# First W_down piece in DMAs of 8, 8 and 112 rows, and c and x in DMAs of odd row counts, in a decode block on one core

## The chip, the cores and the metric

The kernel runs on one core of a Trainium2 chip. The metric is device time in microseconds (us) of one execution. Times below are medians of the runs in the fast state unless said otherwise. (In the slow state an execution is over 1.5% above the fastest of the same kernel.) The profile of the kernel before is of one further execution of 440.03 us.

## The reference

One decode step of a transformer block for 8 batch rows, with adaptive layer norm (six modulation vectors from `c`), grouped-query attention over a cache, and a gated ReLU MLP. Cut to what matters:

```python
mod = (silu(c) @ w_mod)                      # 1024 x 6144
h = layernorm(x) * (1 + ca) + sa
x = x + ga * attention(h, k_cache, v_cache, wq, wo)   # caches: 8 x 4 x 8192 x 128 each
h = layernorm(x) * (1 + cb) + sb
gate, up = h @ W_gate, h @ W_up              # 1024 x 3584 each
x = x + gb * (((gate > 0) * gate * up) @ W_down)      # 3584 x 1024
```

There are only 8 rows of activations, so nearly all the work is reading 185.6 MB of bf16 caches and weights from HBM once.

## The kernel before

All large loads pass through one ring in SBUF (`arena`), in a fixed order: w_mod, wq, then K and V of 16 pairs, wo, W_gate and W_up in two pieces each, W_down in five pieces that get smaller. Each load is one DMA over 128 partitions. They are issued from one queue, as far ahead as the ring has room:

```python
def pump():
    while stream:
        key, src, n = stream[0]
        lo = cursor[0] if cursor[0] + n <= RING else 0
        if P.unread("arena", lo, lo + n):
            return
        ...                                   # cut
        dst = arena[:, lo:lo + n]
        ...                                   # cut
        P.op("sp", lambda e, dst=dst, src=src: e.dma_start(dst, src), writes=[slot_r(lo, lo + n)], dma=True)
...                                           # cut
d_src = B_W_down.rearrange("(p k) n -> p (k n)", k=KF)      # 28 rows of W_down in each partition
...
wd_parts = [(0, 14), (14, 21), (21, 25), (25, 27), (27, 28)]
for i, (r0, r1) in enumerate(wd_parts):
    load(("wd", i), d_src[:, r0 * D:r1 * D], (r1 - r0) * D)
```

So the first W_down piece has 128 rows of 28 KB, the others rows of 14, 8, 4 and 2 KB. A "row" below is what one partition gets from one DMA; in the trace it is one packet (128 packets of 14336 bytes for the second W_down piece, 640 of 28672 for the five loads with 28 KB rows). `c` and `x` are 32 rows of 512 bytes each, queued behind the first half of w_mod.

## Time and profile before

| | before |
|---|---|
| median of 3 runs, the slow one of 446.05 included | 439.97 us (439.25 to 446.05) |
| profiled span | 438.7 us |
| HBM read | 185.6 MB, 423 GB/s over the span |
| a 32 KB row / a 28 KB row on its engine (packet records) | 1.213 us / 1.062 us |
| last W_down piece landed | 435.4 us |

From the page of the kernel before: the span; the busy share of the 16 DMA engines in 40 slices, in tenths; what they moved in each slice; the queues; and the chain that ended last, by engine and by line.

```profile
span 438.7 us, 4012 instructions
DMA  8999999999999999999999999999999999999994
GB/s 359 433 421 444 436 433 429 434 430 429 430 433 430 429 430 430 432 436 434 436 432 433 445 432 430 430 430 432 430 429 428 430 432 437 434 430 430 431 425 180
q1 hardware_dynamic: 6896, 185.64, 98.4%
q8 instruction: 13, 0.21, 0.2%
PE 35%; DMA 32%; DVE 26%; ACT 4%; issue 2%; SPq 1%
PE ps L482 18%; DMA arena<-in_A_k_cache_dram 15%; PE ps L439 13%; DVE kt L428 10%; DMA arena<-in_A_wq_dram 9%; DMA arena<-in_B_W_down_dram 8%; DVE pT L473 7%; DVE negm L446 4%; ACT prb L466 4%; PE ps L452 1%; PE ps L571 1%; DVE mj L457 1%; PE ps L375 1%; PE ps L592 1%; DVE mjt L460 1%
```

The DMA engines are busy from the first slice to the last, at about 430 GB/s. The chain names PE first, but from the first K on a load is issued 25 us and more before it lands (medians by tensor, 25.1 to 36.0 us), so the DMA engines never run dry for long on account of PE. What counts is the end, in the timeline of the kernel before (start, duration, engine, line, operation; in brackets the idle time of the engine before it and what ended that):

```profile
417.49 3.18 PE L592 MATMUL ps<-arena,hT 128*32 128x448 bf16 x32 [5.27 <-DMA arena<-in_B_W_up_dram]
425.96 2.98 PE L610 MATMUL ps<-arena,kt 128*32 128x256 bf16 x56 [5.30 <-DMA arena<-in_B_W_down_dram]
430.26 0.95 PE L610 MATMUL ps<-arena,kt 128*32 128x256 bf16 x28 [1.32 <-DMA arena<-in_B_W_down_dram]
433.63 1.04 PE L610 MATMUL ps<-arena,kt 128*32 128x256 bf16 x16 [2.42 <-DMA arena<-in_B_W_down_dram]
434.86 1.02 PE L610 MATMUL ps<-arena,kt 128*32 128x256 bf16 x12 [0.18 <-DMA arena<-in_B_W_down_dram]
435.93 0.42 DVE L614 TENSOR_TENSOR lu<-ps,mod 128x256 f32<-128x256 f32 x1 [12.25 <-PE ps L610]
```

Every group of matmuls waits for its DMA. After the last piece only a fixed tail is left.

The semaphore of each of these loads gets 16 updates, read here as one from each engine; those of the last piece spread over 4.08 us.

### The profile page before, as it was taken

What the parts mean: (1) busy time and instruction counts of PE and PEld (TensorE: products, weight loads), DVE (VectorE), ACT (ScalarE), POOL (GpSimd) and SP (SyncE); (2) the same over time, 40 slices, a digit from 0 to 9 for tenths busy, and PEclk for the clock granted to TensorE, in tenths of its full rate; (3) what the DMA queues carried; (4) which work ended last, traced back from release to release, by engine and by line L of the source; (5) the groups of instructions that cost most, each with busy time, mean ns of one, the idle gap of its engine ahead of it and who ended that gap; (6) DMA issues with size and microseconds to landing.
All of it is one profiled execution on the core that took longest, in us unless ns stands there. A gap on an engine that the chain in (4) does not pass through costs nothing.

```text
span 438.7 us, 4012 instructions
## 1 busy us (share of the span) xinstructions
PE 271.6 (62%) x1691; PEld 121.2 (28%) x1691; DVE 263.6 (60%) x372; ACT 28.8 (7%) x48; POOL 19.8 (5%) x77
## 2 busy tenths in 40 slices
PE   0053446759595866859586776859586685655243
PEld 0021112324242332324233332424233242342021
DVE  0143057787687867778596867869687878430020
ACT  1100012010101011010101001010101101100000
POOL 6000010000000000000000000000000000000000
PEclk9997669697888969698796968888798978685556
DMA  8999999999999999999999999999999999999994
GB/s 359 433 421 444 436 433 429 434 430 429 430 433 430 429 430 430 432 436 434 436 432 433 445 432 430 430 430 432 430 429 428 430 432 437 434 430 430 431 425 180
DMA packets 6946, 185.90 MB, mean 424 GB/s; under 512 B 816, under 2 KB 912, under 8 KB 1168
## 3 DMA queue, kind: packets, MB, share of 16 engines
q1 hardware_dynamic: 6896, 185.64, 98.4%
q8 instruction: 13, 0.21, 0.2%
q14 instruction: 5, 0.04, 0.0%
q10 hardware_dynamic: 32, 0.01, 0.0%
HBM read 185.63 MB, written 0.02 MB: 423 GB/s over the span
## 4 chain that ended last, share of the span: by engine, by line
PE 35%; DMA 32%; DVE 26%; ACT 4%; issue 2%; SPq 1%
PE ps L482 18%; DMA arena<-in_A_k_cache_dram 15%; PE ps L439 13%; DVE kt L428 10%; DMA arena<-in_A_wq_dram 9%; DMA arena<-in_B_W_down_dram 8%; DVE pT L473 7%; DVE negm L446 4%; ACT prb L466 4%; PE ps L452 1%; PE ps L571 1%; DVE mj L457 1%; PE ps L375 1%; PE ps L592 1%; DVE mjt L460 1%
## 5 line engine op out<-in xcount | busy, mean ns | idle before, releaser
L428 DVE STREAM_TRANSPOSE kt<-arena 128x1024 uint32<-128x1024 uint32 x128 | 149.1, 1215 | 40.4 <-DMA arena<-in_A_k_cache_dram 33.1
L439 PE MATMUL ps<-kt,qpad 128*128 128x512 bf16 x512 | 120.8, 382 | 10.0 <-DVE kt L428 8.7
L482 PE MATMUL ps<-arena,pT 128*64 128x512 bf16 x512 | 94.0, 547 | 51.1 <-DVE pT L473 51.1
L482 PEld LDWEIGHTS ps<-arena,pT 128*64 128x64 bf16 x512 | 44.8, 155 | 94.5 <-issue 89.7
L439 PEld LDWEIGHTS ps<-kt,qpad 128*128 128x128 bf16 x512 | 45.5, 97 | 83.7 <-DVE kt L428 26.5
L473 DVE STREAM_TRANSPOSE pT<-prb 64x1024 bf16<-64x1024 bf16 x32 | 39.6, 1239 | 15.9 <-ACT prb L466 15.4
L466 ACT ACTIVATE prb<-ps,bias 128x1024 bf16<-128x1024 f32 x16 | 17.8, 1113 | 275.0 <-DVE mjt L460 275.0
L446 DVE TENSOR_REDUCE negm<-ps 128x1 f32<-128x512 f32 x32 | 22.1, 689 | 11.7 <-PE ps L439 11.7
L421 POOL COPY qpad<-qR 32x32 bf16<-32x32 bf16 x64 | 13.0, 203 | 308.2 <-PE ps L439 253.8
L592 PE MATMUL ps<-arena,hT 128*32 128x448 bf16 x128 | 12.7, 577 | 14.5 <-DMA arena<-in_B_W_up_dram 6.8
L452 PE MATMUL ps<-identf,negm 128*128 128x128 f32 x32 | 7.8, 325 | 15.7 <-DVE negm L450 15.7
L495 DVE SCALAR_TENSOR_TENSOR om<-ps,im,om 128x128 f32<-128x128 f32 x48 | 16.7, 347 | 0.6
L599 DVE TENSOR_TENSOR kt<-ps,kt 128x448 bf16<-128x448 f32 x2 | 1.2, 619 | 25.0 <-PE ps L592 25.0
L500 PE MATMUL ps<-jmp,om 128*128 128x16 f32 x32 | 6.5, 279 | 14.7 <-DVE om L495 14.7
L375 PE MATMUL ps<-arena,hT 128*32 128x512 bf16 x64 | 6.9, 608 | 13.9 <-DMA arena<-in_A_wq_dram 13.9
L290 DVE CAST cxr<-ps 128x512 bf16<-128x512 f32 x1 | 0.7, 692 | 19.6 <-PE ps L288 19.6
L288 PE MATMUL ps<-cx,rsel 32*128 32x512 bf16 x1 | 0.6, 581 | 19.0 <-DMA cx<-in_A_x_dram 19.0
L610 PE MATMUL ps<-arena,kt 128*32 128x256 bf16 x112 | 6.0, 372 | 9.2 <-DMA arena<-in_B_W_down_dram 9.2
L452 PEld LDWEIGHTS ps<-identf,negm 128*128 128x128 f32 x32 | 4.7, 186 | 23.6 <-DVE negm L450 22.1
L385 DVE CAST kt<-ps 128x512 bf16<-128x512 f32 x1 | 0.7, 692 | 17.2 <-PE ps L375 17.2
L592 PEld LDWEIGHTS ps<-arena,hT 128*32 128x32 bf16 x128 | 4.5, 139 | 22.0 <-DMA arena<-in_B_W_up_dram 8.4
L500 PEld LDWEIGHTS ps<-jmp,om 128*128 128x128 f32 x32 | 5.0, 195 | 18.0 <-DVE om L495 16.9
(80 smaller groups left out, 94.7 us busy)
## 6 DMA issues: line engine op xcount, KB each, us to landing
arena<-in_A_k_cache_dram SPq DMA_DIRECT2D x16, 4096.0 KB, 28.2
arena<-in_A_v_cache_dram SPq DMA_DIRECT2D x16, 4096.0 KB, 25.1
arena<-in_w_mod_dram SPq DMA_DIRECT2D x2, 6144.0 KB, 17.8
arena<-in_A_wq_dram SPq DMA_DIRECT2D x2, 4096.0 KB, 20.0
arena<-in_A_wo_dram SPq DMA_DIRECT2D x2, 4096.0 KB, 26.9
arena<-in_B_W_gate_dram SPq DMA_DIRECT2D x2, 3584.0 KB, 29.4
arena<-in_B_W_up_dram SPq DMA_DIRECT2D x2, 3584.0 KB, 32.5
arena<-in_B_W_down_dram SPq DMA_DIRECT2D x1, 3584.0 KB, 36.0
```

The costliest lines, as they stand in the source:

```text
L375: fns.append(lambda e, w=w, z=z, g=g, kk=kk: e.matmul(ps[32 * g:32 * g + 32, 3 + z, :], hT[:, kk, :], w[:, g, z, :], start=(kk == 0), stop ...
L421: P.op("pool", lambda e, n=2 * m + Q // 2, Q=Q: e.tensor_copy(qpad[32 * Q:32 * Q + 32, m % 2, :, 24 + 32 * Q:32 + 32 * Q], qR[32 * Q:32 * ...
L428: P.op("dve", lambda e: e.transpose(ktb[:, to:to + QE].bitcast(dt.uint32), arena[:, lo:lo + QE].bitcast(dt.uint32)), reads=[slot_r(lo, lo ...
L439: fns.append(lambda e, t=t, r=r: e.matmul(ps[:, b, :].rearrange("p (c k) -> p c k", k=32), qpad[:, m % 2, t * 2 + r, 24 - 8 * i:152 - 8 * ...
L446: P.op("dve", lambda e: e.tensor_reduce(negm[:, h:h + 1], ps[:, b, :], AX.X, ALU.max, negate=True), reads=[bank(b)], writes=[R("negm", h, ...
L452: P.op("pe", lambda e: e.matmul(ps[:, 4, 0:128], negm[:, 2:3].to_broadcast([128, 128]), identf[:], start=True, stop=True), reads=[R("negm" ...
L466: P.op("act", lambda e: e.activation(prb[:], ps[:, 2 * z:2 * z + 2, :].rearrange("p h n -> p (h n)"), ACT.Exp, bias=bias[:, z:z + 1], scal ...
L473: P.op("dve", lambda e, g=g: e.transpose(pT[64 * g:64 * g + 64, z, :, g, :], prb[64 * g:64 * g + 64, :]), reads=[R("prb"), R("pT", z, z + ...
L482: fns.append(lambda e, t=t: e.matmul(ps[64 * (t % 2):64 * (t % 2) + 64, 5, :].rearrange("p (i d) -> p i d", d=Dh), pT[:, z, t].rearrange(" ...
L495: P.op("dve", lambda e, i=i: e.scalar_tensor_tensor(out=om[:], in0=ps[:, 5, Dh * i:Dh * i + Dh], scalar=im[:, i:i + 1], in1=om[:], op0=ALU ...
L500: P.op("pe", lambda e: e.matmul(ps[:, 6, 16 * m:16 * m + 16], om[:], jmp[:].rearrange("p g j -> p (g j)"), start=True, stop=True), reads=[ ...
L592: fns.append(lambda e, w=w, r=kk - r0, kk=kk, h=h, j=j, b0=b0: e.matmul(ps[32 * j:32 * j + 32, b0 + h, 0:H], hT[:, kk, :], w[:, r, j, h, : ...
```

## The change

Its intent: let half of the DMA engines carry 9 of the rows of the first W_down piece and the other half 7, so that all end together; and give c and x a ramp of row counts over the engines. As far as the traces show it, a DMA of 8 rows runs on 8 engines and one of 112 on 16. The core of the diff (the rest lets one operation hold several DMAs on one semaphore):

```diff
-        def load(key, src, n):
-            stream.append((key, src, n))
+        def load(key, src, n, cuts=(0, 128)):
+            stream.append((key, src, n, cuts))
...
-                P.op("sp", lambda e, dst=dst, src=src: e.dma_start(dst, src), writes=[slot_r(lo, lo + n)], dma=True)
+                P.op("sp", [lambda e, a=a, b=b, lo=lo, n=n, src=src: e.dma_start(arena[a:b, lo:lo + n], src[a:b])
+                            for a, b in zip(cuts, cuts[1:])], writes=[slot_r(lo, lo + n)], dma=True)
...
-            load(("wd", i), d_src[:, r0 * D:r1 * D], (r1 - r0) * D)
+            load(("wd", i), d_src[:, r0 * D:r1 * D], (r1 - r0) * D, (0, 8, 16, 128) if i == 0 else (0, 128))
...
-            P.op("sp", lambda e, t=t, src=src: e.dma_start(cx[:, t, :], src), writes=[R("cx", t, t + 1)], dma=True)
+            cuts = ((0, 13, 24, 31, 32), (0, 15, 24, 29, 32))[t]
+            P.op("sp", [lambda e, t=t, src=src, a=a, b=b: e.dma_start(cx[a:b, t, :], src[a:b])
+                        for a, b in zip(cuts, cuts[1:])], writes=[R("cx", t, t + 1)], dma=True)
```

More of the change, by code (lines that the diff above doesn't have):

```diff
@@ L77, in op @@
         if dma:
-            o["dma"] = self.n_dma
+            o["dma"] = self.n_dma % self.N_DMA_SEMS
             self.n_dma += 1
@@ L100, in plan @@
         count = {e: 0 for e in self.ENGINES}
+        landed = [0] * self.N_DMA_SEMS
         for i, o in enumerate(self.ops):
@@ L103, in plan @@
             if o["dma"] is not None:
-                o["sem"] = ("dma", o["dma"] % self.N_DMA_SEMS)
-                o["val"] = 16 * (o["dma"] // self.N_DMA_SEMS + 1)
+                landed[o["dma"]] += 16 * len(o["fns"])
+                o["sem"] = ("dma", o["dma"])
+                o["val"] = landed[o["dma"]]
             elif o["inc"]:
@@ L126, in emit @@
                 ins = f(e)
-            if o["dma"] is not None:
-                ins.then_inc(sems[o["sem"]], 16)
-            elif o["inc"]:
+                if o["dma"] is not None:
+                    ins.then_inc(sems[o["sem"]], 16)
+            if o["inc"]:
                 ins.then_inc(sems[o["sem"]], 1)
@@ L220, in bass_adaLN_cond__gqa_block_cached__glu_gated_reglu__decode_kernel @@
         stream, place, cursor = [], {}, [0]
-        def load(key, src, n):
-            stream.append((key, src, n))
+        def load(key, src, n, cuts=(0, 128)):
+            stream.append((key, src, n, cuts))
         def pump():
             while stream:
-                key, src, n = stream[0]
+                key, src, n, cuts = stream[0]
                 lo = cursor[0] if cursor[0] + n <= RING else 0
@@ L233, in pump @@
                 place[key] = lo
-                dst = arena[:, lo:lo + n]
-                if len(src.shape) == 3:
-                    dst = dst.rearrange("p (a n) -> p a n", a=src.shape[1])
-                P.op("sp", lambda e, dst=dst, src=src: e.dma_start(dst, src), writes=[slot_r(lo, lo + n)], dma=True)
+                P.op("sp", [lambda e, a=a, b=b, lo=lo, n=n, src=src: e.dma_start(arena[a:b, lo:lo + n], src[a:b])
+                            for a, b in zip(cuts, cuts[1:])], writes=[slot_r(lo, lo + n)], dma=True)
         wm_src = w_mod.rearrange("(p k) n -> p (k n)", k=KC)
```

## The prediction

> **What bounds the kernel now.** DMA. The page's slices show the DMA engines at 9 tenths in all but the first and last. In the packet records a 32 KB row takes 1.213 us and a 28 KB row 1.062 us on its engine, practically without spread, so each engine runs at 27.0 GB/s; 185.6 MB over 16 engines at that rate take 429.5 of the 438.7 us. The chain of waits ends with the W_down pieces: the last of them lands at 435.4 us, then matmuls, two DVE operations (0.42 us each) and the output stores, 3.3 us in all. So the last engine's finish sets the time, not the mean.
>
> **Where engines differ.** A DMA's semaphore gets one update per engine, so the landings show skew. The 16 updates of the first load lie within 1.4 us; those of the last piece are, from its first: 0, 0.14, 0.23, 0.26, 0.44, 0.78, 0.85, 1.49, 1.78, 1.88, 2.52, 3.04, 3.05, 3.06, 3.16, 4.08 us. There are 13 instruction packets of 16 KB (DMA queue table), each about 0.95 us, and about each one coincides with one engine dropping back by some 1.5 us. [...]roughly half of the engines are 2 to 3 us behind. Mean lag 1.7 us, worst 4.1 us.
>
> **What the change does.** [...]the 8-row output stores have 9 updates where others have 16. So each 8-row piece puts one row on engines 0 to 7, and the 112-row piece 7 rows on every engine. Against 8 rows now, the low half gains 1.06 us and the high half loses 1.06 us. The c and x rows (0.027 us each, 4 per engine) become a ramp from 8 on engine 0 to 0 on engine 15: 0.1 us either way. SP gains 8 issues of 0.4 us; loads are issued over 25 us ahead and W_mod streams until 16.8 us, so that is hidden.
>
> **Worth.** If the laggards are the high half, the last landing moves from 4.08 to about 3.0: -1.0 us, all on the critical chain. If they are the low half: +1.1 us.
>
> **The risk.** [...]+6 to +13 us. I give this about 0.4.
>
> **Prediction.** 439.5 us, range 438.0 to 449.5; faster by over 2%: 0.01, within 2%: 0.78, slower by over 2%: 0.21.
>
> **What would show it.** Right: W_down rows of 28 KB stay at 1.06 us and the last piece's landings close up to about 3 us or less. Port sharing: those rows take 2 to 4 us and first W_down lands many us later.
>
> **What would make it wrong.** Laggards not lying in one half; instruction packets falling on other engines; port sharing milder or harsher.

The forecast came to 439.5 us, in a range of 438.0 to 449.5. "Port sharing" is the name for the theory that engines slow one another when they write certain SBUF partitions at one time; nothing in the traces is called a port. "Engines 0 to 7" or the low half are the engines that a DMA of 8 rows runs on.

## More of the kernel before

The stage, by stretches of 8 us (engines' busy time, granted clock, DMA share, GB/s):

```profile
420.00:428.00 8.00, 2.70 (x48) 1.59 (x44) 2.85 (x3) 0.00 (x0) 0.00 (x0) 0.50 0.97 417
428.00:436.00 8.00, 3.95 (x80) 1.86 (x72) 0.07 (x1) 0.00 (x0) 0.00 (x0) 0.71 0.58 237
```

The second stretch is where the engines run out of work one after another: the share is 0.58. That unevenness is what the change is after.

## The result

| | before | after |
|---|---|---|
| median of 6 runs (before: with the slow one of 446.05; the five fast ones have 439.32) | 439.57 us (439.2 to 446.05) | 454.19 us (452.31 to 455.39) |
| profiled span | 438.7 us | 453.5 us |
| median 28 KB row of the first W_down piece | 1.06 us | 2.09 us |
| last matmuls start | 434.86 us | 449.59 us |

The changed kernel is slower: ratio 1.0328, 95% interval 1.0297 to 1.036. Ratios here are the mean time of one kernel's fast runs over that of the other's of the same rounds, so not quite the ratio of the medians quoted. The time lies outside the predicted range (438.0 to 449.5).

From the page of the changed kernel:

```profile
span 453.5 us, 4020 instructions
DMA  8999999999999999999999999999999999999993
GB/s 347 445 419 438 431 436 435 423 439 432 425 439 429 436 431 431 432 439 428 432 431 431 438 428 434 436 432 431 429 434 431 435 431 437 421 434 326 229 227 134
q1 hardware_dynamic: 6944, 185.64, 98.1%
q8 instruction: 13, 0.21, 0.2%
PE 43%; DVE 29%; DMA 20%; ACT 5%; issue 2%; SPq 1%
PE ps L484 21%; PE ps L441 16%; DMA arena<-in_B_W_down_dram 11%; DVE kt L430 10%; DVE pT L475 9%; DMA arena<-in_A_k_cache_dram 6%; DVE negm L448 5%; ACT prb L468 4%; DMA cx<-in_A_x_dram 3%; PE ps L454 2%; PE ps L354 2%; PE ps L573 1%; DVE mj L459 1%; PE ps L594 1%; DVE mjt L462 1%
```

Two rows here would mislead. In the DMA row the engines look as busy as before. In the chain the share of DMA falls, from 32% to 20%, although it is DMA that got slower: the attention stage has PE, DVE and DMA close together, and the chain takes another way through it; only the W_down entry, 8% and now 11%, tells of the change. The GB/s row shows the loss: 36 slices are about as before, then come 326, 229 and 227. The engines hold packets but move half the bytes. Timeline and stretches of the same part:

```profile
421.56 3.17 PE L594 MATMUL ps<-arena,hT 128*32 128x448 bf16 x32 [9.26 <-DMA arena<-in_B_W_up_dram]
441.93 3.18 PE L612 MATMUL ps<-arena,kt 128*32 128x256 bf16 x56 [17.20 <-DMA arena<-in_B_W_down_dram]
445.93 1.68 PE L612 MATMUL ps<-arena,kt 128*32 128x256 bf16 x28 [0.81 <-DMA arena<-in_B_W_down_dram]
448.35 1.05 PE L612 MATMUL ps<-arena,kt 128*32 128x256 bf16 x16 [0.75 <-DMA arena<-in_B_W_down_dram]
449.59 1.01 PE L612 MATMUL ps<-arena,kt 128*32 128x256 bf16 x12 [0.19 <-DMA arena<-in_B_W_down_dram]
450.66 0.42 DVE L616 TENSOR_TENSOR lu<-ps,mod 128x256 f32<-128x256 f32 x1 [22.91 <-PE ps L612]
```

```profile
420.00:428.00 8.00, 3.17 (x32) 1.08 (x32) 2.85 (x3) 0.00 (x0) 0.00 (x0) 0.50 0.98 219
428.00:436.00 8.00, 0.00 (x0) 0.00 (x0) 0.00 (x0) 0.00 (x0) 0.00 (x0) 0.50 1.00 208
```

PE now waits 17.20 us for the first W_down piece instead of 5.30. Even the last W_up piece, which the change does not touch, comes 4.1 us later (421.56 against 417.49). Its first landing is where it was (414.26 against 414.29 us), its last one is late (421.52 against 417.44), and the first update of a W_down piece came at 416.89 us. So some engines carried W_down rows while others still had W_up rows. In the packet records the loss can be summed: over all packets, what they took beyond the time of their size in the kernel before, divided by 16 engines, is 8.8 us for the last 128 rows of 28 KB (nearly all of them W_down), 1.2 us for the W_up rows before them and 2.9 us for the 14 KB rows of the second W_down piece, 13 us in all. The mean landing of the last piece moved by as much, 13.2 us. The last landing moved by 14.7 us, because the landings also spread wider, 6.89 us instead of 4.08. That is the +14.7 us at the last matmuls.

### The profile page after: what moved, and what is told of

Read it like the earlier page. It is cut to its first block, busy times and chain, and to the rows that moved or that the text cites. A ratio compares the mean times of both kernels' runs of the same rounds, so it can differ in the third digit from the quotient of the medians.

```text
span 453.5 us, 4020 instructions
## 1 busy us (share of the span) xinstructions
PE 273.6 (60%) x1691; PEld 122.4 (27%) x1691; DVE 263.9 (58%) x372; ACT 28.8 (6%) x48; POOL 19.9 (4%) x77
## 4 chain that ended last, share of the span: by engine, by line
PE 43%; DVE 29%; DMA 20%; ACT 5%; issue 2%; SPq 1%
PE ps L484 21%; PE ps L441 16%; DMA arena<-in_B_W_down_dram 11%; DVE kt L430 10%; DVE pT L475 9%; DMA arena<-in_A_k_cache_dram 6%; DVE negm L448 5%; ACT prb L468 4%; DMA cx<-in_A_x_dram 3%; PE ps L454 2%; PE ps L354 2%; PE ps L573 1%; DVE mj L459 1%; PE ps L594 1%; DVE mjt L462 1%
## 5 line engine op out<-in xcount | busy, mean ns | idle before, releaser
L502 PE MATMUL ps<-jmp,om 128*128 128x16 f32 x32 | 6.7, 286 | 14.7 <-DVE om L497 14.7
```

## The experiments

Theories:

- **Sharing on the write side** ("port sharing"). Engines that write certain partitions of SBUF at one time slow one another. In the kernel before, with DMAs of 128 rows, the last 128 rows of 28 KB all took 1.062 us; DMAs of other row counts may bring engines together. Which partitions share, and the model of engines worked out from it, were my assumption and were not shown.
- **Rival 1, unequal counts.** 9 against 7 rows, with engines as the only limit: about 1 us either way.
- **Rival 2, the DMAs as such.** More or smaller DMAs, or row counts that are no power of two, are slow in themselves.
- **Rival 3, the read side.** The HBM addresses read at one time collide.

The kernels derive from the changed one. The list of cuts was made general, with destination rows, source rows and columns; `W0` is the list for the first W_down piece, and in all but the second run c and x are whole again:

```diff
+                P.op("sp", [lambda e, d=d, s=s, a=a, b=b, lo=lo, src=src: e.dma_start(arena[d, lo + a:lo + b], src[s, a:b])
+                            for d, s, a, b in cuts], writes=[slot_r(lo, lo + n)], dma=True)
```

The results in one table; "before" was run beside each (medians 439.24 to 439.64 us). The row column is the median time of the last 128 packets of 28 KB in the profiled run.

| run | first W_down piece | us | ratio to before | 28 KB row, us |
|---|---|---|---|---|
| e2_cx_only | one DMA of 128 | 439.45 | 1.000 | 1.06 |
| e4_cols3 | three DMAs of 128, by columns | 439.6 | 1.000 | (24 KB: 0.91) |
| e3_wd_only | 8, 8, 112 | 454.1 | 1.032 | 2.12 |
| e6_r16_112 | 16, 112 | 452.1 | 1.030 | 2.16 (slow state) |
| e5_halves | 64, 64 | 451.7 | 1.027 | 2.17 |
| e8_eight_far | 16 of 8 rows, 4 apart | 449.5 | 1.023 | 1.06 |
| e10_far_from_near | as e8, source rows neighbours | 449.4 | 1.023 | 1.06 (slow state) |
| e7_eight_near | 16 of 8 neighbouring rows | 458.8 | 1.041 | 1.70 |
| e9_near_from_far | as e7, source rows 4 apart | 457.9 | 1.043 | 1.61 |
| e11_eight_pair | 16 of 8 rows, 8 apart | 462.8 | 1.054 | 2.12 |
| e12_shift | 2 KB of each row by 16 DMAs of 8 rows, rest 128 | 442.0 | 1.006 | (own sizes) |

Runs in the slow state (458.63 of e6, 462.88 of e7, 465.88 of e9, 456.54 of e10) are left out. e9 and e10 put W_down rows in the wrong partitions on purpose; they passed the comparison with the reference all the same, so its tolerance does not see this.

### Which part: e2_cx_only and e3_wd_only

```diff
-cuts = ((0, 13, 24, 31, 32), (0, 15, 24, 29, 32))[t]      # e3: as in the kernel before
+cuts = (0, 32)
-(0, 8, 16, 128) if i == 0 else (0, 128)                   # e2: one DMA of 128 rows
+(0, 128)
```

> Only the c and x part of the change; W_down in one piece of 128 rows. Every theory that blames the W_down pieces expects the kernel before within 0.5 us (439 to 440 us), row times of 1.06 us at 28 KB. If the eight small loads cost anything by themselves, it shows here as +1 us or more.

> Only the W_down part (8, 8 and 112 rows), c and x whole. Sharing of write ports, and any other theory that blames these pieces: 452 to 455 us, as the whole change, with 28 KB rows at 2 us and more. A theory of unequal row counts alone (9 against 7 rows of 1.06 us): 438.5 to 441 us.

Measured 439.45 us (ratio 1.000, interval 0.9987 to 1.0012) and 454.1 us. The c and x part does nothing measurable; the whole loss is in the W_down pieces. Rival 1, 9 against 7 rows at unchanged row times, falls here: rows take 2.12 us.

### The DMAs as such: e4_cols3, e6_r16_112 and e5_halves

```diff
+W0 = [(slice(0, 128), slice(0, 128), a, b) for a, b in ((0, 1024), (1024, 2048), (2048, n0))]   # e4
+W0 = [(slice(a, b), slice(a, b), 0, n0) for a, b in ((0, 16), (16, 128))]                       # e6
+W0 = [(slice(a, b), slice(a, b), 0, n0) for a, b in ((0, 64), (64, 128))]                       # e5
```

> The first W_down piece in three DMAs again, but cut by columns: 128 rows each of 2, 2 and 24 KB. Three DMAs on one semaphore, 24 rows per engine instead of 8[...]. Port sharing: no loss, 439 to 440.5 us, row times as their bytes at 27 GB/s. If it is the number of DMAs or of packets that costs: 445 us or more.

> The first W_down piece in DMAs of 16 and 112 rows: 1 + 7 rows, so 8 for every engine, no imbalance, but the same 112-row piece. Unequal counts as the cause: back to 439.5 us. Port sharing: [...]by the model 447 to 451 us; what is left to the measured 454 is the part of the two 8-row pieces.

> The first W_down piece in two DMAs of 64 rows each; every engine takes 4 + 4 rows, as many as before. Port sharing[...]: [...]rows at about 2.1 us, and[...] 445 to 447 us. Unequal row counts alone: 439.5 us. A cost of each DMA under 128 rows that is due to odd counts such as 7 per engine: 439.5 us, since 64 is a power of two.

Three DMAs cost nothing while each spans 128 partitions (439.6 us). With 16 and 112 rows every engine has 8 again, if they are divided evenly, and the time stays at 452.1 us: the imbalance is not the cause. Two halves of 64 rows, no odd count anywhere, cost 12 us. In stretches of the halves:

```profile
426.00:434.00 8.00, 0.00 (x0) 0.00 (x0) 2.03 (x2) 0.00 (x0) 0.00 (x0) 0.65 0.98 206
```

All 16 engines are busy (0.98) and move 206 GB/s, a little under eight times one engine's 27 (28 KB in 1.062 us). So odd counts are not needed for the loss. The row time met its forecast (rows of "about 2.1 us" came at 2.17), but my model's times for e5 (445 to 447) and e6 (447 to 451) were too low.

### Neighbours or not, with the same engines: e7_eight_near, e8_eight_far, e11_eight_pair

```diff
+W0 = [(slice(8 * i, 8 * i + 8), <same>, 0, n0) for i in range(16)]                              # e7: 0 1 2 ... 7
+W0 = [(slice(b, b + 29, 4), <same>, 0, n0) for b in (0..3, 32..35, 64..67, 96..99)]             # e8: 0 4 8 ... 28
+W0 = [(slice(b, b + 57, 8), <same>, 0, n0) for b in (0..7, 64..71)]                             # e11: 0 8 16 ... 56
```

(The lists are written short here.) In all three, 16 DMAs of 8 rows carry the piece, on 8 engines (DMA share 0.49 in e7 and 0.50 in e11 from 434 to 442 us, 0.50 in e8 from 426 to 434 us) with 16 rows each, if divided evenly.

> The first W_down piece in 16 DMAs of 8 neighbouring rows, all on engines 0 to 7: 16 rows each instead of 8. Engines alone: 8 rows of 1.06 us more, 446 to 448.5 us. Port sharing: [...]rows at up to 4.2 us; by the model 470 to 480 us[...].

> The same 16 DMAs of 8 rows on engines 0 to 7, but the 8 rows are every fourth one (0, 4, ... 28 and so on)[...]. Port sharing: rows at 1.06 us, 446 to 448.5 us, that is over 20 us faster than with neighbouring rows. If small or odd DMAs are slow by themselves, both take the same time.

> 16 DMAs of 8 rows on engines 0 to 7 again, rows 8 apart (0, 8, ... 56 and so on). [...]rows well over 1.06 us (up to 2.1), time between 450.5 and 460. If only nearness of the rows counted, it would be as with rows 4 apart: 449.5 us, rows of 1.06 us.

Stretches of e8 and then of e11, at a time when the 8 engines carry 28 KB rows of the first piece and the other engines are done (in e8 from 427.8 us on):

```profile
426.00:434.00 8.00, 0.00 (x0) 0.00 (x0) 0.00 (x0) 0.00 (x0) 0.00 (x0) 0.50 0.50 192
```

```profile
434.00:442.00 8.00, 0.00 (x0) 0.00 (x0) 0.00 (x0) 0.00 (x0) 0.00 (x0) 0.50 0.50 106
```

Both have half of the 16 engines busy. With rows 4 apart they move 192 GB/s, 24 for each of 8 engines; with rows 8 apart 106 GB/s, 13 for each, and rows take 2.12 us and not 1.06. Engines, DMA count and bytes are the same. The source rows in HBM are 8 apart too, and in e11, as in e5, that was not separated from the destination. This is the clearest comparison. Partitions 4 to 28 apart within one group of 32 do not slow one another (e8), and 0, 8, 16 and 24 are such partitions, as are 32, 40, 48 and 56. If it is the destination, then, it is rows of one group of 32 and rows of the other that meet in e11; which with which, and by what, the runs do not show.

Neighbouring rows are slow too, 458.8 us, but not as slow as my model had it (470 to 480): rows took 1.70 us and not 4. Why they did was not shown. e11 ended above my range (462.8 against at most 460).

e8 was 1 us above its range, and its packet records tell when. Of its 128 rows 23, all started between 422.4 and 427.5 us, took 1.27 to 2.16 us. The other 8 engines were then still at their last pieces, whose 2 KB rows took up to 0.18 us and not 0.084. When these were done, rows took 1.06 us again. Both were slow at the same time; by what was not shown.

One thing more. In e7, e11 and e9 (which follows below) the other 8 engines went on to 64 rows of 14 KB of the second piece (half of its 128) while the 8-row DMAs were still running. These rows took 0.91, 0.97 and 0.83 us in the mean; in e8 and e10 all 64 took 0.535 us. So where the 8-row DMAs were slow, rows on the other engines were slow as well. How that comes about is open.

### Write side or read side: e9_near_from_far and e10_far_from_near

```diff
+W0 = [(slice(8 * i, 8 * i + 8), slice(b, b + 29, 4), 0, n0) for ...]      # e9: to neighbours, from rows 4 apart
+W0 = [(slice(b, b + 29, 4), slice(8 * i, 8 * i + 8), 0, n0) for ...]      # e10: the other way round
```

> Wrong result on purpose. 16 DMAs of 8 rows on engines 0 to 7; the 8 destination partitions are neighbours (as in the run with neighbouring rows, 458.8 us), the 8 source rows in HBM are every fourth one (as in the run with rows 4 apart, 449.5 us). If the write side[...] is what is shared: as with neighbouring rows, 455 to 463 us and 28 KB rows of 1.4 to 2 us. If the read side (HBM addresses) is: about 449.5 us and 1.06 us.

> Wrong result on purpose. The other way round: destination partitions 4 apart, source rows neighbours. Write side shared: 448.5 to 451 us, rows of 1.06 us. Read side shared: 455 to 463 us, rows of 1.4 to 2 us.

e9 took 457.9 us like e7 (458.8), e10 449.4 us like e8 (449.5). The time follows the destination partitions and not the addresses in HBM. Rival 3 falls for these row distances.

### Was there anything to balance: e1_marks, e13_marks_again, e12_shift, e14_shift_marks

The marked kernel is the kernel before with 15 tiny loads behind the last piece; the load of k rows is meant to reach k engines and the next load the same and one more. Engines are numbered here in the order in which the marks add them, so that those of a DMA of 8 rows should be 0 to 7 (in e14 these ended 2.5 us later than in e1, the others 0.6):

```diff
+        for k in range(1, 16):
+            P.op("sp", lambda e, k=k: e.dma_start(mk[0:k, 64 * (k - 1):64 * k], c[0:1, 0:64 * k].rearrange("o (p n) -> (o p) n", p=k)),
+                 writes=[("mk", k, k + 1)], dma=True)
```

> The kernel before, with 15 tiny loads of 1 to 15 rows of 128 bytes queued behind the last W_down piece. [...]If the prediction's reading of the skew is right, engines 8 to 15 are the ones that end 1.5 to 4 us late and engines 0 to 7 end within 1.5 us of the first; if the laggards are mixed or in the low half, the intended balance could not have worked either. Time: within 1 us of the kernel before.

> The marked kernel before once more. If lateness belongs to the engine (instruction packets always on the same ones), engines 3, 6 and 9 to 12 are again the last, at 2.6 to 3.3 us after the first, and 0, 2, 4, 7, 8, 15 within 0.6 us. If it is chance, others are late. Only if the late ones lay in the high half in both would 9 and 7 rows be a balance.

The mark of k rows had k landings in the trace, each next one with one more. When each engine was done with the last W_down piece, in us after the first engine, worked out from the landings (a mark's new landing less 0.195 us, the delay of a first mark behind that piece; sorted, these times agree with the 16 landings of the piece itself within 0.03 us):

| engine | 0 | 1 | 2 | 3 | 4 | 5 | 6 | 7 | 8 | 9 | 10 | 11 | 12 | 13 | 14 | 15 |
|---|---|---|---|---|---|---|---|---|---|---|---|---|---|---|---|---|
| e1 | 0.2 | 1.0 | 0.5 | 2.6 | 0.1 | 1.7 | 3.1 | 0.2 | 0 | 3.1 | 3.0 | 3.2 | 3.3 | 1.7 | 2.2 | 0.3 |
| e13 | 0 | 0.7 | 0.5 | 2.5 | 0.1 | 1.4 | 3.3 | 0.1 | 0 | 3.1 | 2.9 | 3.0 | 3.0 | 1.4 | 2.0 | 0.2 |

The same engines are late in both runs (440.21 and 440.28 us, one run each). But they lie in both halves. The high half is later on average (2.1 against 1.2 us in e1), yet engine 6 of the low half is as late as any. A ninth row of 1.06 us on engine 6 would have put the end about 1 us later, not earlier, even with every row at 1.06 us. That is an estimate from these lags; it was not run.

e12 tried the balance in small with rows 4 apart; e14 is the same with marks (one run):

```diff
+W0 = [(slice(b, b + 29, 4), <same>, 0, D) for b in (0..3, 32..35, 64..67, 96..99)] + [(slice(0, 128), slice(0, 128), D, n0)]
```

> What the change wanted, in small and without neighbouring rows: of the first W_down piece the first 2 KB of each partition go in 16 DMAs of 8 rows 4 apart on engines 0 to 7, the other 26 KB in one DMA of 128 rows. Engines 0 to 7 move 16 KB more (0.6 us), engines 8 to 15 16 KB less. If the high half alone were late, and engines alone the limit: -0.6 us. By the marks (engines 3 and 6 are 2.6 and 3.1 us late, 9 to 12 are 3.0 to 3.3): no gain, +0.3 to +1 us.

> The run with 2 KB pieces shifted to engines 0 to 7 (+2.5 us), with marks. If engines alone set the pace and instruction packets fall as before: engine 6 last, 3.7 us and more after the former first, engines 8 to 15 about 0.6 us earlier against 0 to 7. If sharing of ports by the 16 extra pieces[...] is the cost: both halves end 2 to 3 us later than in the kernel before, and 28 KB rows before them are stretched to 1.5 us.

It cost 2.5 us (442.0 us, interval of the ratio 1.0044 to 1.007), more than I had allowed. In e14 the low half ended 2.5 us later than in e1 (mean of engines 0 to 7: 435.0 against 432.5 us after the start), with engine 6 last at 5.1 us after the first. The high half, by the cut with 16 KB less to carry for each engine, ended not 0.6 us earlier but 0.6 us later (434.0 against 433.5). Neither of my two forecasts for e14 fits as written: the halves did not move alike, and only some of the 28 KB rows before were stretched (mean 1.10 us, 95th percentile 1.42). Why the high half gained nothing was not shown. The packet records of e14 account for the loss. Over their usual times the 28 KB rows, the 26 KB rows and the smaller ones took 1.5 us more per engine, 1.1 us of it in the 26 KB rows (mean 1.12 us, median 0.99). The mean of the 16 engines also ended 1.5 us later than in e1. So no cost of each small DMA needs to be added. The marks landed 0.18 us apart on an engine, but their packets followed one another every 0.015 us, and the first 2 KB rows every 0.086 us at 0.084 us each.

## Why the prediction was wrong

- **What bounds the kernel: right.** The stream of DMAs, and the last engine to end. Everything before slice 37 stayed as it was.
- **"c and x ... 0.1 us either way", hidden issues: right within the noise.** e2 took 439.45 us against 439.62 (ratio 1.000, interval 0.9987 to 1.0012); an effect of 0.1 us could not be seen.
- **The step that failed: the weight of the branch.** The prediction said of port sharing "I give this about 0.4" and put its figure at 439.5 us, on the other branch, with row times unchanged. What failed in its terms is that "W_down rows of 28 KB stay at 1.06 us". They took 2.09 us. The runs showed that the write side binds: rows of 2.1 us in place of 1.06 with halves and with rows 8 apart (e5, e11), 1.06 us as the median with rows 4 apart (e8, e10), and a time that follows the destination (e9, e10). The profile of the kernel before could not show it: there all of the last 128 rows took 1.062 us.
- **The size in the other branch: too small.** The figure was "+6 to +13 us", an estimate whose basis was not shown; it was +14.6 us in the medians. The term that was mis-sized is the time in which engines slow one another: all of the last 128 rows took 1.9 us or more (8.8 us per engine), and I had not counted what the W_up rows before (1.2 us) and the 14 KB rows after (2.9 us) lose.
- **"If the laggards are the high half ... -1.0 us": a wrong picture.** I inferred two groups from sorted landings. The marks show late engines in both halves (3, 6, 9 to 12), so there was little to win by this split even without contention. The 4.08 us was also one late landing in one trace: in e1, e2, e4 and e13 the last piece's landings spread over 3.2 to 3.35 us.
- **The cause of the lags** (the 13 instruction packets) was argued from coincidence in time and stays open (at the one of 429.6 us in the kernel before, the longest lag went from 3.21 us in one piece to 4.10 in the next). That the same engines are late in two runs fits a fixed assignment, and is no proof of it.
- **How the 112 rows are divided among the engines** was not seen. That they slow one another is inferred from the row times (2.09 us) and from e6 (2.16 us, slow state).

## What to carry to other kernels

In these runs a row's time depended on which partitions the engines wrote at one time (1.06 us with rows 4 apart in e8, 2.12 with rows 8 apart in e11), and slow rows went with slow rows on other engines too (14 KB in 0.97 us in e11, and not 0.535). The load cut by columns, keeping all 128 partitions, cost nothing (e4, 439.6 us); cut by partitions into halves it ran at half speed (e5, rows of 2.17 us). Shifting rows between engines to even them out did not help (e12, +2.5 us); why was not shown. And find out which engine is late before balancing: sorted landings do not name engines, a few marked loads do.
